# Groups of eight heads in a ring of three 8 MiB slots: fewer, longer loads for a decode attention block that streams its cache

## The chip, the cores and the metric

One core of one Trainium2 chip. The metric is device time in microseconds (us), the median of several executions; lower is better.

## The reference, cut to what matters

Eight requests, one new token each. An attention block over a cache (32 heads, 4096 positions, 128 values per head) and an MLP (576 to 4608 to 576) run on the same input and are mixed by a gate.

```python
q = (x @ wq)                      # (8, 1, 576) @ (576, 4096), 32 heads of 128
scores = einsum("bhqd,bhkd->bhqk", q, k_cache) * 128 ** -0.5
p = softmax(scores)
a = einsum("bhqk,bhkd->bhqd", p, v_cache).reshape(8, 1, 4096) @ wo
b = gelu(layernorm(x) @ w1 + b1) @ w2 + b2
out = g * a + (1 - g) * b         # g = sigmoid(sum(x * gate_w))
```

K and V are 268 MB each, in bf16, and every byte is used once. The weights are another 20 MB.

Of the kernel before, what the change touches and what calls it, by code (L numbers as in the profile page):

```python
# [21 lines left out]
HB = 4  # L22
NHG = H // HB
NG = NHG * B
NTT = SK // 32
# [4 lines left out]
TQ = 4  # L30
QN = D // 4
QP = 96 + B
NTQ = NTT // TQ
# [51 lines left out]
def bass_gated_mix__mha_block_cached__mixer_channel_mlp__decode_kernel(  # L85
# [32 lines left out]
    KB = [sb(f"KB{i}", [128, NTT, DH], BF16) for i in range(2)]  # L118
    VB = [sb(f"VB{i}", [128, NTT, DH], BF16) for i in range(2)]
    RB = sb("RB", [128, 9 * F // 2], BF16)  # L120
    wq_sb = view(RB, 0, [128, 4, SK])
    wq_t = view(RB, 4 * SK, [128, SK // 2])
    w1_sb = view(RB, 0, [128, 4, F])
    w1_t = view(RB, 4 * F, [128, F // 2])
    w2_sb = view(RB, 0, [128, NJ, D])
    wo_sb = view(RB, 0, [128, H, D])
    p1 = sb("p1", [128, 2, CT, DH], BF16)

    pos = [0]

    def early(shape):
        n = int(np.prod(shape[1:]))
        ap = view(p1, pos[0], shape)
        pos[0] += n
        assert pos[0] <= 2 * CT * DH
        return ap

    x_sb = early([B, D])
    gw8 = early([B, D])
    y_sb = early([B, D])  # L140
    junk = early([B, D])
    xz = early([B, 2, 64, 2])
    yz = early([B, 2, 64, 2])
    xT_sb = early([128, NKF + 2, B])
    yT_sb = sb("yT_sb", [128, NKF + 2, B], BF16)
    b1_sb = sb("b1_sb", [128, NJ], BF16)
    b2_4 = sb("b2_4", [128, QN], BF16)
    hT_sb = sb("hT_sb", [128, NJ, B], BF16)
    up = sb("up", [128, 2, NJ * B], F32)
    Q4 = sb("Q4", [128, NHG * DH], BF16)  # L150
    Sel = sb("Sel", [128, B, 128], BF16)
    q_bc = sb("q_bc", [128, 2, DH], BF16)
    OT_sb = sb("OT_sb", [128, H, B], BF16)
    bmg_sb = view(up, 0, [128, QN])
# [3 lines left out]
    ones = sb("ones", [128, 128], F32)  # L158
    sel16 = sb("sel16", [128, TQ, HB], F32)
# [5 lines left out]
    mD = sb("mD", [128, 2, 32], F32)  # L165
    gm = sb("gm", [128, 1], F32)
    P = sb("P", [128, 2, NTT, HB], BF16)
    rs = sb("rs", [128, 2, HB], F32)
    O_sb = sb("O_sb", [128, TQ, DH], F32)
    rz = sb("rz", [128, HB], F32)  # L170
# [7 lines left out]
    up_ps = bank[6]  # L178
    y_ps = bank[7]
    YT_COL = 64  # L180

    sK = [nc.alloc_semaphore(f"sK{i}") for i in range(2)]
    sV = [nc.alloc_semaphore(f"sV{i}") for i in range(2)]
    nK, nV = [0, 0], [0, 0]
# [8 lines left out]
    def bcast(t):  # L193
        return bass.AP(tensor=t.tensor, offset=t.offset, ap=[[0, B], [1, D]])

    c_b2 = op("gpsimd", lambda e: e.memset(b2_4[:], 0.0))
    c_g4 = op("gpsimd", lambda e: e.memset(g4[:], 0.0))
    ld_x = load("sync", x_sb, x_flat, "ld_x")
    ld_gw = load("scalar", gw8, bcast(gate_w), "ld_gw")
    ld_b2 = [load("scalar", b2_4[32 * i:32 * i + B, :],  # L200
                  bass.AP(tensor=B_b2.tensor, offset=B_b2.offset + i * QN, ap=[[0, B], [1, QN]]), f"ld_b2{i}", [c_b2])
             for i in range(4)]
    ld_b1 = load("scalar", b1_sb[:, :], B_b1.rearrange("(p j) -> p j", j=NJ), "ld_b1")
    def halves(w):
# [3 lines left out]
    ld_wq = [load("sync", wq_sb, A_wq[0:512, :].rearrange("(kt p) n -> p kt n", p=128), "ld_wqa"),  # L208
             load("sync", wq_t, halves(A_wq), "ld_wqb")]


    def kv_src(cache, g):
        hg, b = divmod(g, B)
        return cache[b, hg * HB:(hg + 1) * HB].rearrange("h (p t) d -> (h p) t d", p=32)

    k_done, v_done = {}, {}
    k_land, v_land = {}, {}

    def load_k(g):
        s = g % 2  # L220
        nK[s] += 1
        src = kv_src(A_k_cache, g)
        k_land[g] = op("sync", lambda e: e.dma_start(KB[s][:, :, :], src), [k_done.get(g - 2)], dma=(sK[s], 16 * nK[s]))  # L223

    def load_v(g):
        s = g % 2
        nV[s] += 1
        src = kv_src(A_v_cache, g)
        t = op("sync", lambda e: e.dma_start(VB[s][:, :, :], src), [v_done.get(g - 2)], dma=(sV[s], 16 * nV[s]))  # L229
        v_land[g] = [(t, 0, NTT)]  # L230

    V_LAST = (32, 32, 16, 16, 16, 8, 8)

    def load_v_pieces(g):
        s = g % 2
        src = kv_src(A_v_cache, g)
        v_land[g] = []
        t0 = 0
        for n, nt in enumerate(V_LAST):
            dst, part = VB[s][:, t0:t0 + nt, :], src[:, t0:t0 + nt, :]  # L240
            t = load("sync", dst, part, f"sVl{n}", [v_done.get(g - 2)])
            v_land[g].append((t, t0, t0 + nt))
            t0 += nt
        assert t0 == NTT

    load_k(0)
    load_v(0)
    load_k(1)


    def memset(engine, ap, value):
# [7 lines left out]
    c_ones = memset("gpsimd", ones[:], 1.0)  # L259
    c_mA = memset("gpsimd", mA[:], 0.0)  # L260
    c_P = memset("gpsimd", P[:], 0.0)
    c_ps = [memset("vector", bank[i][:, :], 0.0) for i in range(4)]
    c_yps = memset("vector", y_ps[:, :], 0.0)
    c_sel16 = op("vector", lambda e: e.tensor_reduce(
        out=sel16[:].rearrange("p t h -> p (t h)"),
# [3 lines left out]
        out=Sel[:].rearrange("p b (h r) -> p b h r", h=HB),  # L269
        in_=bass.AP(tensor=ident, offset=0, ap=[[pstride(ident), 128], [1, B], [32, HB], [0, 32]])), [c_id])  # L270
# [24 lines left out]
    def transposed(src, srcz, col, waits):  # L295
        last = None
        for kt in range(NKF + 2):
            o = up_ps[:, col + kt * B:col + (kt + 1) * B]
            i = src[:, kt * 128:(kt + 1) * 128] if kt < NKF else srcz[:, kt - NKF, :, :].rearrange("b r s -> b (r s)")
            last = op("tensor", lambda e, o=o, i=i: e.matmul(o, lhsT=i, rhs=ident[0:B, 0:B], start=True, stop=True),  # L300
                      waits if kt == 0 else ())
        return last

    def untransposed(dst, col, waits):
        return op("vector", lambda e: e.tensor_copy(
            out=dst.rearrange("p k b -> p (k b)"), in_=up_ps[:, col:col + (NKF + 2) * B]), waits)

    v_xz = spread(xz, x_sb, [ld_x])
    p_xT = transposed(x_sb, xz, 0, [ld_x, c_id, v_xz])
# [11 lines left out]
    v_yT = untransposed(yT_sb[:, :, :], YT_COL, [p_yT])  # L321
# [3 lines left out]
    for half in range(2):  # L325
        for h in range(HB):
            for kt in range(NKT):
                o = tr_ps[half][32 * h:32 * h + B, :]
                at = (kt * SK + half * (SK // 2) if kt < NKF else NKF * SK) + h * DH
                r = bass.AP(tensor=RB, offset=at, ap=[[pstride(RB), 128], [HB * DH, 4], [1, DH]])  # L330
# [6 lines left out]

    ld_w1 = [load("sync", w1_sb, B_w1[0:512, :].rearrange("(kt p) f -> p kt f", p=128), "ld_w1a", [p_Q]),
             load("sync", w1_t, halves(B_w1), "ld_w1b")]


    a_qb, v_mult, v_red, p_sum, v_nm, a_exp, p_pv, a_ev, p_oz, v_norm, v_rs, p_z, v_rz = ({} for _ in range(13))

    def q_of(g):
        hg, b = divmod(g, B)
        t = op("tensor", lambda e: e.matmul(qb_ps[:, 0:DH], lhsT=Sel[:, b, :], rhs=Q4[:, hg * DH:(hg + 1) * DH],  # L346
                                            start=True, stop=True), [a_Q[hg // 4], c_Sel, a_qb.get(g - 1)])
        a_qb[g] = op("scalar", lambda e: e.activation(out=q_bc[:, g % 2, :], in_=qb_ps[:, 0:DH], func=ACT.Copy),  # L348
                     [t, v_mult.get((g - 2, NCK - 1))])

    def mult(g, c):
        s, par = g % 2, c % 2
        qb = bass.AP(tensor=q_bc, offset=q_bc[:, s, :].offset, ap=[[pstride(q_bc), 128], [0, CT], [1, DH]])
        v_mult[g, c] = op("vector", lambda e: e.tensor_tensor(  # L354
            out=p1[:, par, :, :], in0=KB[s][:, c * CT:(c + 1) * CT, :], in1=qb, op=ALU.mult),
            [k_land[g], a_qb[g], p_sum.get((g, c - 2) if c >= 2 else (g - 1, c + NCK - 2))]
            + ([v_yT, p_yT, p_Q] if g == 0 and c < 2 else []))
        if c == NCK - 1:
            k_done[g] = v_mult[g, c]
        for n in range(NCH):  # L360
            r = bass.AP(tensor=p1, offset=p1[:, par, 0, n * CH:n * CH + 1].offset,
                        ap=[[pstride(p1), 128], [DH, CT], [1, CH]])
            w = [v_mult[g, c], v_red.get((g, c - 2) if c >= 2 else (g - 1, c + NCK - 2)), *a_Q] if n == 0 else ()
# [21 lines left out]
    def softmax(g):  # L385
# [4 lines left out]
        t = op("vector", lambda e: e.tensor_reduce(out=gm[:, :], in_=mB[:, :], axis=AX.X, op=ALU.max), [t])  # L390
        gmb = bass.AP(tensor=gm, offset=0, ap=[[pstride(gm), 128], [0, 32]])
        t = op("vector", lambda e: e.tensor_scalar(out=mC[:, :], in0=gmb, scalar1=-1.0, scalar2=None, op0=ALU.mult), [t])
        v_nm[g] = op("vector", lambda e: e.transpose(mD[:, s, :], mC[:, :]), [t, a_exp.get(g - 2)])  # L393
        for h in range(HB):
            q = slice(32 * h, 32 * h + 32)
            a_exp[g] = op("scalar", lambda e, h=h, q=q: e.activation(  # L396
# [118 lines left out]
    def norm_turned(g):  # L515
# [3 lines left out]
            [p_oz[g], v_rz[g]])  # L519


    UP0, UPN = 3, 12
    DN0, DNN = 19, 6
    AP0 = 28
    q_of(0)
# [107 lines left out]
```

## The kernel before: the parts that the change touches

A group is one request and four heads: 4 MiB of K and 4 MiB of V, in which each of the 128 partitions holds one contiguous row of 32 KiB (128 positions of one head). K and V have two buffers each, and the weights pass one after the other through a fifth buffer.

```python
HB = 4                                   # heads of a group
KB = [sb(f"KB{i}", [128, NTT, DH], BF16) for i in range(2)]
VB = [sb(f"VB{i}", [128, NTT, DH], BF16) for i in range(2)]
RB = sb("RB", [128, 9 * F // 2], BF16)   # wq, then w1, w2, wo
p1 = sb("p1", [128, 2, CT, DH], BF16)    # products of K and q, two chunks
def load_k(g):                           # waits until the products of group g-2 are done
    ...
    op("sync", lambda e: e.dma_start(KB[s][:, :, :], src), [k_done.get(g - 2)], ...)
V_LAST = (32, 32, 16, 16, 16, 8, 8)      # the last V comes in seven pieces
```

Scores are made in chunks of 32 positions per partition: VectorE multiplies the chunk by the query into `p1`, TensorE adds up 8 slices of 16 values with an identity matrix, and VectorE reduces the remaining 16. Softmax, the value product on TensorE, and the normalisation follow, spread over the next groups' chunks by `between`.

```python
def mult(g, c):
    v_mult[g, c] = op("vector", ... tensor_tensor(out=p1[:, par, :, :], in0=KB[s][...], in1=qb, op=ALU.mult) ...)
    for n in range(NCH):                 # 8 matmuls of 512 columns
        ... matmul(tr_ps[par][:, :], lhsT=ident[:, :], rhs=r, ...)
def between(c, g=g):
    if c == 1 and g >= 1:
        rowsum(g - 1)                    # VectorE: sums of the exponentials
        ...
```

## Time and profile before

| | before |
|---|---|
| time, median of the 3 runs made first | 1310.3 us |
| span of the profile | 1308.8 us |
| bytes read | 557 MB, 426 GB/s over the span |
| busy: TensorE / VectorE / ScalarE | 64% / 66% / 16% |

These are lines of the page of the kernel before: the DMA rows of the 40 equal slices of the span (busy share in tenths, then GB/s), and the first lines of its chain of waits.

```profile
DMA  9999999999999999999999999999999999999997
GB/s 398 422 431 432 431 432 431 432 431 430 434 424 432 430 431 429 428 418 432 429 431 429 431 431 431 431 432 430 432 430 431 431 431 429 432 431 432 429 420 311
...
DMA 69%; DVE 20%; PE 10%; SPq 0%; issue 0%; ACT 0%
```

The loads bound the kernel. The DMA engines are busy in nearly every slice, at a rate that hardly moves. Compute engines have a third of their time to spare, so work taken from them is worth nothing by itself. What can be won is in the rate of the stream, its gaps, its start and its end.

This is the view by windows for the kernel before: each row is a stretch in us, then its length, then busy time and instruction counts of PE, PEld, DVE, ACT and POOL, then the granted clock (the share of TensorE's full clock that it was given), the DMA share and GB/s. The view counts a packet wholly in the stretch in which it starts, so a share can come out a little wrong, and even above 1.

```profile
core 0: us, PE busy (x) PEld busy (x) DVE busy (x) ACT busy (x) POOL busy (x), PEclk, DMA share, GB/s
1284.00:1286.00 2.00, 2.00 (x8) 0.68 (x7) 1.38 (x3) 0.00 (x0) 0.00 (x0) 0.62 0.99 426
1286.00:1288.00 2.00, 2.00 (x16) 0.77 (x18) 2.00 (x2) 0.00 (x0) 0.00 (x0) 1.00 0.84 360
1288.00:1290.00 2.00, 2.00 (x31) 0.81 (x24) 2.00 (x3) 0.47 (x1) 0.00 (x0) 1.00 0.53 221
1290.00:1292.00 2.00, 1.61 (x9) 0.57 (x7) 2.00 (x2) 0.13 (x1) 0.00 (x0) 1.00 0.79 291
1292.00:1294.00 2.00, 2.00 (x14) 1.27 (x12) 0.61 (x2) 0.00 (x0) 0.00 (x0) 1.00 0.92 373
```

The DMA share falls to 0.53. The prediction below comes to this dip.

### The profile page before, as it was taken

How to read it: one execution, taken by the hardware profiler on the slowest of the kernel's cores; microseconds unless marked ns; L12 is line 12 of the kernel's file. 1: busy time of each engine (PE TensorE's matmuls, PEld its weight loads, DVE VectorE, ACT ScalarE, POOL GpSimd, SP SyncE). 2: the span in 40 equal slices, each digit the busy share in tenths (PEclk: the TensorE clock that was granted, in tenths of full speed). 3: DMA queues.
4: the chain of work that ended last, by engine and by line, in shares of the span. 5: the costliest groups of instructions: out<-in, count | busy, mean ns of one | idle time of the engine just before them, and what ended most of it. 6: DMA issues, size and time to landing. Idle time of an engine off the chain costs nothing.

```text
span 1308.8 us, 12641 instructions
## 1 busy us (share of the span) xinstructions
PE 843.5 (64%) x5428; PEld 384.4 (29%) x5428; DVE 869.7 (66%) x1061; ACT 204.1 (16%) x393; POOL 2.5 (0%) x13
## 2 busy tenths in 40 slices
PE   3567766766746666646766766765766665766766
PEld 1223433433312233212322222322322222322323
DVE  4576676676747667646766766766776666776675
ACT  1201111111210110101011111011111111111111
POOL 0000000000000000000000000000000000000000
PEclk8878888878868888768878878878878878878878
DMA  9999999999999999999999999999999999999997
GB/s 398 422 431 432 431 432 431 432 431 430 434 424 432 430 431 429 428 418 432 429 431 429 431 431 431 431 432 430 432 430 431 431 431 429 432 431 432 429 420 311
DMA packets 25255, 557.77 MB, mean 426 GB/s; under 512 B 2528, under 2 KB 6640, under 8 KB 7536
## 3 DMA queue, kind: packets, MB, share of 16 engines
q1 hardware_dynamic: 24944, 556.95, 99.4%
q8 instruction: 42, 0.69, 0.2%
q14 instruction: 13, 0.11, 0.0%
q10 hardware_dynamic: 256, 0.03, 0.0%
HBM read 556.96 MB, written 0.01 MB: 426 GB/s over the span
## 4 chain that ended last, share of the span: by engine, by line
DMA 69%; DVE 20%; PE 10%; SPq 0%; issue 0%; ACT 0%
DMA KB<-in_A_k_cache_dram 68%; DVE p L354 16%; PE psb L364 10%; DVE s_sb L369 3%; DMA VB<-in_A_v_cache_dram 1%; SPq L187 0%; PE psb L414 0%; ACT L467 0%; SPq L229 0%; DVE mA L387 0%; SPq L223 0%; PE psb L477 0%; DVE mB L389 0%; ACT O_sb L427 0%; DVE gm L390 0%
## 5 line engine op out<-in xcount | busy, mean ns | idle before, releaser
L364 PE MATMUL psb<-p,ident 128*128 128x512 bf16 x2048 | 610.9, 459 | 412.2 <-DVE p L354 411.8
L354 DVE TENSOR_TENSOR p<-KB,q_bc 128x4096 bf16<-128x4096 bf16 x256 | 579.6, 2285 | 278.0 <-DMA KB<-in_A_k_cache_dram 278.0
L364 PEld LDWEIGHTS psb<-p,ident 128*128 128x128 bf16 x2048 | 218.1, 114 | 744.5 <-DVE p L354 445.2
L369 DVE TENSOR_REDUCE s_sb<-psb 128x32 f32<-128x512 f32 x256 | 176.1, 688 | 129.9 <-PE psb L364 129.6
L427 ACT ACTIVATE O_sb<-psb 128x512 f32<-128x512 f32 x63 | 37.6, 597 | 1032.2 <-PE psb L414 1032.2
L396 ACT ACTIVATE P<-s_sb,mD 32x128 bf16<-32x128 f32 x256 | 147.0, 574 | 12.9 <-DVE mD L393 9.0
L414 PE MATMUL psb<-VB,P 128*16 128x512 bf16 x2016 | 119.9, 379 | 0.3 <-DMA VB<-in_A_v_cache_dram 0.3
L432 PE MATMUL psb<-sel,O_sb 128*128 128x4 f32 x504 | 66.9, 256 | 32.9 <-ACT O_sb L427 32.9
L432 PEld LDWEIGHTS psb<-sel,O_sb 128*128 128x128 f32 x504 | 61.6, 192 | 41.3 <-ACT O_sb L427 41.2
L414 PEld LDWEIGHTS psb<-VB,P 128*16 128x16 bf16 x2016 | 44.7, 89 | 70.4 <-issue 26.3
L402 DVE TENSOR_REDUCE rs<-P 128x4 f32<-128x512 bf16 x64 | 43.5, 680 | 2.1 <-ACT P L396 2.1
L421 PEld LDWEIGHTS psb<-rs,ones 128*128 128x128 f32 x128 | 24.4, 192 | 9.3 <-issue 0.4
L348 ACT ACTIVATE q_bc<-psb 128x128 bf16<-128x128 f32 x64 | 17.4, 272 | 32.7 <-PE psb L346 32.7
L452 PEld LDWEIGHTS psb<-yT_sb,RB 128*128 128x128 bf16 (+1 forms) x216 | 19.4, 165 | 3.4
L452 PE MATMUL psb<-yT_sb,RB 128*128 128x8 bf16 (+1 forms) x216 | 19.8, 227 | 0.0
L387 DVE TENSOR_REDUCE mA<-s_sb 128x1 f32<-128x128 f32 x64 | 18.3, 286 | 2.2
L421 PE MATMUL psb<-rs,ones 128*128 128x4 f32 x128 | 18.4, 214 | 0.0
L389 DVE STREAM_TRANSPOSE mB<-mA 128x32 f32<-128x32 f32 x64 | 13.6, 213 | 2.2
L393 DVE STREAM_TRANSPOSE mD<-mC 128x32 f32<-128x32 f32 x64 | 13.6, 212 | 2.2
L346 PE MATMUL psb<-Q,Sel 128*128 128x128 bf16 x64 | 14.7, 229 | 0.0
L346 PEld LDWEIGHTS psb<-Q,Sel 128*128 128x128 bf16 x64 | 6.1, 96 | 27.0 <-issue 26.8
L390 DVE TENSOR_REDUCE gm<-mB 128x1 f32<-128x32 f32 x64 | 11.9, 186 | 2.2
(63 smaller groups left out, 84.7 us busy)
## 6 DMA issues: line engine op xcount, KB each, us to landing
KB<-in_A_k_cache_dram SPq DMA_DIRECT2D x64, 4096.0 KB, 27.2
VB<-in_A_v_cache_dram SPq DMA_DIRECT2D x63, 4096.0 KB, 33.1
RB<-in_B_w_dram SPq DMA_DIRECT2D x1, 5184.0 KB, 44.3
RB<-in_B_w_dram SPq DMA_DIRECT2D x1, 4608.0 KB, 36.6
RB<-in_A_wo_dram SPq DMA_DIRECT2D x1, 4608.0 KB, 44.7
RB<-in_A_wq_dram SPq DMA_DIRECT2D x1, 4096.0 KB, 12.8
VB<-in_A_v_cache_dram SPq DMA_DIRECT2D x2, 1024.0 KB, 8.7
VB<-in_A_v_cache_dram SPq DMA_DIRECT2D x3, 512.0 KB, 11.2
```

The source lines that it names most:

```text
L346: t = op("tensor", lambda e: e.matmul(qb_ps[:, 0:DH], lhsT=Sel[:, b, :], rhs=Q4[:, hg * DH:(hg + 1) * DH], start=True, stop=True), [a_Q[hg ...
L354: v_mult[g, c] = op("vector", lambda e: e.tensor_tensor(out=p1[:, par, :, :], in0=KB[s][:, c * CT:(c + 1) * CT, :], in1=qb, op=ALU.mult), ...
L364: p_sum[g, c] = op("tensor", lambda e, r=r, n=n: e.matmul(tr_ps[par][:, :], lhsT=ident[:, :], rhs=r, start=(n == 0), stop=(n == NCH - 1)), w)
L369: v_red[g, c] = op("vector", lambda e: e.tensor_reduce(out=s_sb[:, s, c * CT:(c + 1) * CT], in_=tr_ps[par][:, :].rearrange("p (t c) -> p t ...
L387: t = op("vector", lambda e: e.tensor_reduce(out=mA[:, 0:1], in_=s_sb[:, s, :], axis=AX.X, op=ALU.max), [v_red[g, NCK - 1], c_mA])
L396: a_exp[g] = op("scalar", lambda e, h=h, q=q: e.activation(out=P[q, s, :, h], in_=s_sb[q, s, :], func=ACT.Exp, bias=mD[q, s, 0:1], scale=1.0),
L402: v_rs[g] = op("vector", lambda e: e.tensor_reduce(out=rs[:, s, :], in_=P[:, s, :, :].rearrange("p t h -> p h t"), axis=AX.X, op=ALU.add), ...
L414: p_pv[g] = op("tensor", lambda e, o=o, tq=tq: e.matmul(o, lhsT=P[:, s, tq * TQ:(tq + 1) * TQ, :].rearrange("p t h -> p (t h)"), rhs=VB[s] ...
L421: p_z[g] = op("tensor", lambda e: e.matmul(oz_ps[:, HB:2 * HB], lhsT=ones[:, :], rhs=rs[:, g % 2, :], start=True, stop=True), [v_rs[g], v_ ...
L427: a_ev[g] = op("scalar", lambda e: e.activation(out=O_sb[:].rearrange("p t d -> p (t d)"), in_=o_ps[s][:, :], func=ACT.Copy), [p_pv[g], p_ ...
L432: p_oz[g] = op("tensor", lambda e, tt=tt: e.matmul(oz_ps[:, 0:HB], lhsT=O_sb[:, tt, :], rhs=sel16[:, tt, :], start=(tt == 0), stop=(tt == ...
L452: st["p_up"] = op("tensor", lambda e, w=w, o=o, kt=kt: e.matmul(o, lhsT=w, rhs=yT_sb[:, kt, :], start=(kt == 0), stop=(kt >= NKF)), [*ld_w ...
```

## The change

Intent: a group takes eight heads, so that a row is 64 KiB and a load 8 MiB, half as many and twice as long. To have room for that, K, V and all weights share one ring of three 8 MiB slots, and the product of K and the query is written over K in place. The MLP is done first, while the first K and V stream in. wo is loaded last. The diff, cut to its core:

```diff
-HB = 4
+HB = 8
-    KB = [sb(f"KB{i}", [128, NTT, DH], BF16) for i in range(2)]
-    VB = [sb(f"VB{i}", [128, NTT, DH], BF16) for i in range(2)]
-    RB = sb("RB", [128, 9 * F // 2], BF16)
-    p1 = sb("p1", [128, 2, CT, DH], BF16)
+    SL = sb("SL", [128, 3 * SLOT], BF16)
+    slot = [view(SL, i * SLOT, [128, NTT, DH]) for i in range(3)]
...
+    def load_kv(kind, g):
+        n = n_load[0]
+        s = n % 3
+        ...
+        land[kind, g] = op("sync", lambda e: e.dma_start(slot[s][:, :, :], src), free[n - 3], dma=(sS[s], 16 * nS[s]))
...
-        v_mult[g, c] = op("vector", ... tensor_tensor(out=p1[:, par, :, :], in0=KB[s][...], in1=qb, op=ALU.mult),
+        v_mult[g, c] = op("vector", ... tensor_tensor(out=part, in0=part, in1=qb, op=ALU.mult),
...
         def between(c, g=g):
-            if c == 1 and g >= 1:
+            if g >= 1 and c == 1:
                 rowsum(g - 1)
...
         scores(g, between)
+        free[n_of["k", g]] = [p_sum[g, NCK - 1]]
+        if g < NG - 1:
+            next_load()
+        else:
+            load_wo(free[n_of["k", g]])
+        if g >= 1:
+            pv(g - 1)
+            free[n_of["v", g - 1]] = [p_pv[g - 1]]
+            next_load()
         softmax(g)
+        if g >= 1:
+            evict(g - 1)
```

The loads come in the order K0, K1, V0, K2, V1, K3, V2 and so on. Load n waits for the slot of load n-3. The probabilities `P` have one buffer instead of two, so the exponentials of a group wait for the value product of the group before.

## The prediction

> **What bounds the kernel now.** The loads. The page's slice rows show the DMA engines 90% or more busy in 39 of 40 slices, at 430 to 432 GB/s in most; PE is busy 64%, DVE 66%. The DMA view gives 557 MB in a span of 1308.8 us. In the trace's packet records a 32 KiB packet takes 1.216 us on one of 16 engines (431 GB/s in all), back to back from about 3.4 to 1304.5 us. The Trainium skill, "DMA: Bandwidth & Descriptors", section "Where 436 GB/s comes from", states a ceiling of 435; this trace agrees. So streaming has under 1% left, and compute saved is off the path: DVE waits 278 us for K loads (waits view).
>
> Not at full rate: 3 us before the first packets; 4096 wo packets of 1152 B (13.1 us per engine instead of about 11); near the end two 2 us stretches at 74% and 57%, where the last V's pieces wait for an earlier product (1.5 us lost), then small V packets; 4.3 us from the last packet to the end.
>
> **What the change does.** Same bytes.
> - 64 KiB rows: from packets of 32768 B (1.216 us) and 41472 B (1.538 us) I estimate 2.428 us for 65536 B, against 2.432 for two of 32 KiB: 2 us saved.
> - wo in rows of 4608 B: 1.5 to 2 us saved. wq, w1 in long rows: under 1 us.
> - Last V whole, no dip: 1.5 to 2 us saved; wo (about 11.5 us) streams last and hides the last product with V.
> - Longer tail: after the last wo bytes come gather, normalise, transpose and 32 output matmuls; I estimate 5.7 us instead of 4.3.
> - Per group of eight heads: 8 chunks of 2.28 (product) + 0.69 (reduce) plus about 4: 28 us DVE per two loads (38.9 us). The exponentials took 0.57 us for 128 columns; at 256 I estimate 1 us, 8 us per group on ACT: it fits.
> - Ring of three: a K slot must be free within two loads of landing. Scores take about 27 us, slack 11, so the queue should never run dry.
> - MLP first: w1 lands about 27 us, up about 6, gelu 4, 144 small transposes 8, down 4 to 10: done near 55 us; its slot is wanted about 78, and K of group 0 lands about 59. No bubble; least slack about 4 us, for the second K's slot, about 115 us.
>
> **Sum.** Start 3 us, packets about 1292, tail about 5.7: span about 1301, time (1.5 above the span, as before) about 1303 us, 0.6% faster.
>
> Predicted 1303 us, 8 in 10 between 1298 and 1309. Faster by over 2%: 0.02. Within 2%: 0.93. Slower by over 2%: 0.05.
>
> **What would show it.** K and V packets of 65536 B at 2.42 to 2.44 us; slices at 430 to 433 GB/s with no dip at wo or near the end; wo packets of 4608 B; a chain of waits that ends in wo; DVE waiting for K about 10 us per group; MLP done before 60 us.
>
> **What would make it wrong.** (1) 64 KiB rows put the engines' streams 512 KiB apart instead of 256; the same page ("Latency and other measured facts") reports much slower copies at some power-of-two row pitches. No trace here shows it; if it strikes, packets exceed 2.5 us and the time rises several per cent. (2) Slots freed late: three buffers only, and in-place products hold K until the last PE sum; each 1 us missed per group costs 32 us. (3) The MLP ends after 78 us. (4) The tail chain runs over 8 us.

## The result, and the profile after

| | before | after |
|---|---|---|
| time, median (lowest to highest) | 1310.5 us (1310.3 to 1310.7, 4 runs) | 1307.5 us (1307.0 to 1307.7, 4 runs) |
| span of the profile | 1308.8 us | 1305.3 us |
| first byte of the large loads to the last | 1.7 to 1304.3 us | 1.8 to 1300.8 us |
| last byte to the end | 4.6 us | 4.5 us |
| typical K/V packet | 32 KiB, 1.216 us | 64 KiB, 2.421 us |
| mean granted TensorE clock | 0.82 | 0.85 |

The ratio is 0.9977 with a 95% interval of 0.9963 to 0.9991. The change is 3.0 us faster where 7 were predicted. The measured time lies in the predicted range, but only because the range was wide: less than half of the forecast gain came.

These lines of the page after answer to those of before: the DMA rows of the slices, and the head of the chain of waits.

```profile
DMA  9998999999999999999999999999999999999997
GB/s 392 437 440 376 436 432 433 433 432 434 428 440 426 437 432 432 436 426 441 422 443 424 441 424 437 430 438 426 440 424 441 424 440 427 438 431 432 432 436 299
...
DMA 53%; DVE 30%; PE 13%; ACT 4%; issue 0%; SPq 0%; ACTq 0%
```

There is a dip that was not there before: 376 GB/s in the fourth slice, 98 to 131 us. In the view by windows no packet starts in it from 116 to 120 us (same columns as above):

```profile
112.00:114.00 2.00, 1.62 (x9) 0.59 (x7) 2.00 (x2) 0.28 (x1) 0.00 (x0) 1.00 0.68 295
114.00:116.00 2.00, 1.66 (x8) 0.70 (x8) 2.00 (x3) 0.00 (x0) 0.00 (x0) 1.00 1.14 492
116.00:118.00 2.00, 1.10 (x6) 0.41 (x5) 1.69 (x2) 0.00 (x0) 0.00 (x0) 1.00 0.00 0
118.00:120.00 2.00, 2.00 (x25) 0.85 (x27) 0.89 (x2) 0.00 (x0) 0.00 (x0) 1.00 0.00 0
```

The trace also has every DMA packet. By these records the engines ran dry one after the other, from 116.2 to 118.2 us, and began again from 120.0 to 120.9 us; all 16 stood still together for 1.9 us. A load ends with 16 small packets, one for each engine, so their times tell when each engine was done with it. For the loads around the dip:

```
load   first engine done   last engine done   since the load before
K0          58.2                60.1               19.7
K1          77.5                79.5               19.3
V0          96.9                98.8               19.4
K2         116.2               118.2               19.4
V1         139.9               141.4               23.3
K3         159.2               160.8               19.4
```

An 8 MiB load takes 19.35 us when the stream is full. V1 is 3.9 us late, and nothing later makes up for it. V1 needs the slot of K1. This is the timeline of the kernel after for the scores of group 1 on VectorE and ScalarE (start, duration, engine, line, operation; in brackets the idle time before it and what ended it):

```profile
87.45 4.48 DVE L437 TENSOR_TENSOR SL<-SL,q_bc 128x4096 bf16<-128x4096 bf16 x2
87.58 9.42 ACT L477 ACTIVATE P<-s_sb,hb 128x256 bf16<-128x256 f32 x8 [6.21 <-DVE hb L474]
97.03 2.29 DVE L482 TENSOR_REDUCE rr<-P 128x1 f32<-128x2048 bf16 x1 [5.09 <-ACT P L477]
99.23 0.68 DVE L447 TENSOR_REDUCE s_sb<-psb 128x32 f32<-128x512 f32 x1
```

VectorE makes two products of group 1 and then stands idle for 5.1 us. Its next instruction is the row sum of group 0 (L482), which needs all eight exponentials of group 0 (L477), and these take 9.4 us. K1 has been there since 79.5 us. The engine that frees the slot is blocked by an instruction that has nothing to do with the slot. The waits view of the kernel after shows that this happens only four times (total us, times, longest). By the timeline these are groups 1 to 4, with 5.1, 6.4, 3.0 and 1.5 us, and only the first of them made a load late:

```profile
DVE SL L437 <- DMA SL<-in_A_k_cache_dram: 255.3, 29, 10.9
...
DVE rr L482 <- ACT P L477: 15.9, 4, 6.4
```

The same packet records show a second thing. The spread between the first and the last of the 16 engines at the end of a load grows through the run: 1.5 us at V1, 3.5 us near 550 us, 7.7 us at 1270 us. At the end, with the last of wo, seven engines were done by 1293.1 to 1295.1 us and nine only by 1299.1 to 1300.7 us. The average engine finished at 1297.1 us, 3.7 us before the last.

### The profile page after: what moved, and what is told of

Same layout as the page of the kernel before. It is cut to its first block, busy times and chain, and to the rows that moved or that the text cites. A ratio compares the mean times of both kernels' runs of the same rounds, so it can differ in the third digit from the quotient of the medians. Undisturbed runs are those within 1.5% of the kernel's fastest.

```text
span 1305.3 us, 11677 instructions
## 1 busy us (share of the span) xinstructions
PE 739.7 (57%) x5136; PEld 302.2 (23%) x5136; DVE 880.3 (67%) x860; ACT 329.6 (25%) x330; POOL 3.8 (0%) x19
## 4 chain that ended last, share of the span: by engine, by line
DMA 53%; DVE 30%; PE 13%; ACT 4%; issue 0%; SPq 0%; ACTq 0%
DMA SL<-in_A_k_cache_dram 51%; DVE SL L437 21%; PE psb L442 6%; PE psb L492 5%; DVE s_sb L447 5%; ACT P L477 4%; DVE rr L482 3%; DMA SL<-in_A_wo_dram 2%; PE psb L510 1%; DMA SL<-in_A_wq_dram 1%; DVE Orow L517 0%; PE psb L355 0%; DVE rz L516 0%; PE psb L506 0%; PE psb L406 0%
## 5 line engine op out<-in xcount | busy, mean ns | idle before, releaser
L442 PE MATMUL psb<-SL,ident 128*128 128x512 bf16 x2048 | 559.8, 426 | 521.4 <-DVE SL L437 521.4
L437 DVE TENSOR_TENSOR SL<-SL,q_bc 128x4096 bf16<-128x4096 bf16 x256 | 581.5, 2282 | 267.1 <-DMA SL<-in_A_k_cache_dram 255.3
L442 PEld LDWEIGHTS psb<-SL,ident 128*128 128x128 bf16 x2048 | 200.9, 107 | 855.2 <-DVE SL L437 608.2
L477 ACT ACTIVATE P<-s_sb,hb 128x256 bf16<-128x256 f32 x256 | 299.9, 1602 | 296.1 <-PE psb L492 289.9
L492 PE MATMUL psb<-SL,P 128*32 128x512 bf16 x2048 | 118.2, 383 | 0.0
L482 DVE TENSOR_REDUCE rr<-P 128x1 f32<-128x2048 bf16 x32 | 73.0, 2280 | 16.0 <-ACT P L477 15.9
L492 PEld LDWEIGHTS psb<-SL,P 128*32 128x32 bf16 x2048 | 54.2, 97 | 60.9 <-issue 13.1
L510 PE MATMUL psb<-O_sb,sel 128*8 128x128 f32 x256 | 34.4, 279 | 9.9 <-ACT O_sb L498 9.9
L510 PEld LDWEIGHTS psb<-O_sb,sel 128*8 128x8 f32 x256 | 21.2, 91 | 14.5 <-ACT O_sb L498 10.0
L465 DVE TENSOR_REDUCE mA<-s_sb 128x1 f32<-128x256 f32 x32 | 13.4, 420 | 1.1
```

Source lines behind the costliest of these rows:

```text
L437: v_mult[g, c] = op("vector", lambda e: e.tensor_tensor(out=part, in0=part, in1=qb, op=ALU.mult), [land["k", g], a_qb[g]])
L442: p_sum[g, c] = op("tensor", lambda e, r=r, n=n: e.matmul(tr_ps[par][:, :], lhsT=ident[:, :], rhs=r, start=(n == 0), stop=(n == NCH - 1)), w)
L465: t = op("vector", lambda e: e.tensor_reduce(out=mA[:, 0:1], in_=s_sb[:, s, :], axis=AX.X, op=ALU.max), [v_red[g, NCK - 1], c_mA])
L477: a_exp[g] = op("scalar", lambda e, h=h: e.activation(out=P[:, :, h], in_=s_sb[:, s, :], func=ACT.Exp, bias=hb8[:, h:h + 1], scale=1.0), [ ...
L482: v_rs[g] = op("vector", lambda e: e.tensor_reduce(out=rr[:, g % 2:g % 2 + 1], in_=P[:, :, :].rearrange("p t h -> p (t h)"), axis=AX.X, op ...
L492: p_pv[g] = op("tensor", lambda e, o=o, tq=tq: e.matmul(o, lhsT=P[:, tq * TQ:(tq + 1) * TQ, :].rearrange("p t h -> p (t h)"), rhs=vb[:, tq ...
```

## The experiments

Two things had to be explained: the 3.9 us gap, and the slow drift of the engines. The first theory is the blocked row sum; its rivals are that three slots are too few in any case, or that the MLP delays the first scores. For the drift, one suspect is the instruction fetches: the records of the DMA engines also hold packets of the kind "instruction", 40 of 16 KiB in TensorE's queue in the kernel after and some of 8 KiB in another. The other suspect is engines or memory places that differ in speed. A third question is what the 64 KiB rows are worth alone. Each experiment was timed against the kernel before in the same rounds; that one's median was between 1310.5 and 1310.6 us in every set, so medians of different sets can be compared to about 0.2 us. The three sets (e1 to e4, e5 to e7, e8 to e10) ran on three chips.

### e1: the row sum later

```diff
-            if g >= 1 and c == 1:
+            if g >= 1 and c == 5:
                 rowsum(g - 1)
```

> Only the row sum moves, from the second to the sixth chunk of the next group's scores. Theory (in the first groups, where K has already landed, VectorE stands idle in the row sum until the eight exponentials of the group before are done, so the second K's slot is freed late and the queue runs dry for 3.9 us): the gap in the load completions between the fifth and the sixth K/V load shrinks from 23.3 to 19.4 us, and the time falls by 3 to 4 us against the changed kernel, to about 1303.8 us. Rival (three slots are too few whatever VectorE does, or the MLP holds up the first scores): the gap stays, and the time stays within 1 us of 1307.5.

Measured: 1305.06 us (1304.6 to 1306.2, 5 runs), 2.5 us faster than the change. V1 came 19.8 us after K2 instead of 23.3. So the gap was made by the blocked row sum and not by the three slots or the MLP. The time gained less than the gap, and the runs scattered over 1.6 us: something else now had a part in the end. In the profile, the end came 5.8 us after the last byte instead of 4.5.

### e2: more instructions on TensorE

e1 with each value product cut in two of 256 columns.

```diff
-            p_pv[g] = op(... o, lhsT=P[...], rhs=vb[:, tq * TQ:(tq + 1) * TQ, :] ...)
+            for u in range(2):
+                p_pv[g] = op(... o[:, 256 * u:256 * u + 256], lhsT=P[...], rhs=vb[:, tq * TQ + 2 * u:tq * TQ + 2 * u + 2, :] ...)
```

> e1 with each of the 2048 value products on TensorE cut into two of 256 columns: same arithmetic and same K and V bytes, 4096 more TensorE instructions. Theory (the instruction fetches take about 1 us each on the same nine or ten of the 16 DMA engines, so these fall behind the other six, and the end is set by the slowest): about 16 more fetch packets of 16 KiB, the spread of the 16 engines at the last K/V load grows from about 7.6 to 9.5 to 11 us, and the time is 1.5 to 3 us above e1. Rival (the spread comes from engines that differ in speed or from where the rows lie in memory): spread within 0.7 us of that of e1, time within 0.5 us of e1 unless the first groups stall again.

Measured: 1309.22 us, 4.2 us slower than e1, with 16 more fetch packets of 16 KiB. The direction is the theory's and the size is above it. The spread did not grow as expected: it was 5.9 us at the last K/V load and 4.8 at the one before, because the engines that were ahead ran out of freed slots (the first engine's completions came up to 2.4 us late in five loads). As the end also came 6.3 us after the last byte, e2 does not separate the fetches from the extra work on TensorE. It was repeated as e9 on a cleaner base.

### e3: half rows

e1 with every K/V load issued as two loads of half the positions.

```diff
+        for u in range(2):
+            nS[s] += 1
+            ts = slice(u * NTT // 2, (u + 1) * NTT // 2)
+            ... e.dma_start(slot[s][:, ts, :], src[:, ts, :]) ...
```

> e1 with each K/V load issued as two of 4 MiB, so the packets are 32 KiB again and everything else is as in e1. If longer packets are worth what the two traces say (2 x 1.216 against 2.421 us a packet, 512 packets an engine): 4 to 6 us slower than e1. By the estimate in the prediction (2.432 against 2.428): 2 us slower. If the length of a packet does nothing: 0.

Measured: 1310.35 us, 5.3 us slower than e1, as the packets' durations say and more than the prediction's 2 us. But its end came 6.8 us after the last byte, so part of that may be the end. It was repeated as e10.

### e4: which engines are late

e1 with a tiny load of 2 to 14 rows behind each K/V load. The Trainium skill, "DMA: Bandwidth & Descriptors", section "Why a DMA increments its semaphore by 16 and not by 1", says that a load over fewer rows runs on the lowest-numbered engines. The trace has one packet for each row of these loads, as that asks, but no record shows an engine's number.

```diff
+        mark_at[i] = op("sync", lambda e: e.dma_start(mark[0:kk, i, 0:w], A_wq[0:kk, 0:w]), ...)
```

> e1 with a tiny load of 2 to 14 rows behind each K/V load, which by the page on DMA uses only the lowest-numbered engines; the moment of its packets tells which engines are the late ones. Theory: the same six engines are ahead in all loads. If the low-numbered ones are ahead, the marks of 2 to 6 rows come with the first completions of their load; if they are behind, 6 us after the first. Time within 1 us of e1.

Measured: 1307.12 us in the one execution, 2 us above e1, so the expected 1 us was missed. The markers worked: each came within 0.03 us of a completion of its load. At the last marked loads, the 2-row marker sat 0.5 and 2.1 us behind the first engine, the 4-row marker added one engine near the first and one 4.8 us behind, and the 6-row marker again one of each. So both readings fail: if the page is right about the numbers, the low-numbered engines are neither the early nor the late ones, but mixed. Bytes can then not be shifted to the early ones by the number of rows alone.

### e5: the last value products earlier

e1 with the value product of the last group but one, and its eviction, ahead of the last chunk of scores.

```diff
+            if c == 6 and g == NG - 1:
+                pv(g - 1)
+                evict(g - 1)
```

> e1 with, in the last group only, the value product of the group before and its eviction moved ahead of the last chunk of scores, so that the last exponentials (9.4 us) start about 1.7 us earlier and the last value product no longer waits behind a gather that waits for the eviction. Theory (in e1 the last value product starts at 1289.8 us although its data landed about 1285.7, and the output products end about 2 us after the last wo piece): the last value product starts about 2.5 us earlier, the time falls by 1.5 to 2 us against e1, and then the wo loads end the kernel. Rival (the wo loads already end it): within 0.5 us of e1.

Measured: 1306.84 us, with runs from 1303.8 to 1307.9. A miss: not faster than e1. The profiled run (the slowest, 1307.9) shows why. The product did not wait for V, which had landed at 1268.7 us; it ran from 1276.0 to 1279.6 us. But TensorE works in order, and now the sums of the last chunk come behind the product, from 1279.6 us, and VectorE's maximum behind them. In e1 the maximum was made while the product ran. So the last exponentials started at 1283.9 us instead of 1279.2. Part of that is chance in this run: K31 landed 1.8 us later, and the sums before the product took 3.4 us instead of 1.9, at a granted clock of 0.50. Work moved forward in an in-order queue delays what it passes by its own length.

### e6: the row sum last

e1 with the row sum behind the last product, so that it delays neither the slot nor anything that the slot waits for.

```diff
-            if g >= 1 and c == 5:
+            if g >= 1 and c == 7:
                 rowsum(g - 1)
```

> e1 with the row sum behind the last product instead of the sixth, so that each K slot comes free about 2.3 us earlier. In e1 the engines that run ahead were short of work three times (0.5 to 1.8 us) because no slot was free for them. If the slowest engines set the end: the engines ahead get further ahead (spread at the last K/V load 7 to 9 us instead of 5.5), and the time stays within 0.7 us of e1. If the ring's slack sets it: faster by 1.5 us or more.

Measured: 1303.19 us (1303.17 to 1303.36, 5 runs), 1.9 us faster than e1, 4.3 us faster than the change, and 0.9944 of the kernel before (0.9930 to 0.9957). It is the fastest version that computes the reference. The expectation does not decide it: by its time the rival won (faster by over 1.5 us), by its spread the theory (7.9 us at the last K/V load, and the first engine no longer late there). Both left out the end of the kernel, and the profiles of e1 and e6 show it. The last K/V byte came at 1285.7 us in e1 and 1285.6 in e6, the last byte of all at 1297.1 and 1296.9, so the stream was no faster. But from the last byte to the end it took 5.8 us in e1 and 4.5 in e6. This is e1, then e6, with the row sum of the last group but one, its value product, the start of the last group's exponentials (eight in all, but the views end at 1281 us), and the last line of the chain of waits:

```profile
1265.64 2.28 DVE L482 TENSOR_REDUCE rr<-P 128x1 f32<-128x2048 bf16 x1
...
1275.40 3.64 PE L492 MATMUL psb<-SL,P 128*32 128x512 bf16 x64
...
1279.15 2.56 ACT L477 ACTIVATE P<-s_sb,hb 128x256 bf16<-128x256 f32 x2 [28.67 <-PE psb L492]
...
1290.43 4.71 PE psb L492 x54
```

```profile
1270.98 2.28 DVE L482 TENSOR_REDUCE rr<-P 128x1 f32<-128x2048 bf16 x1
1272.95 3.64 PE L492 MATMUL psb<-SL,P 128*32 128x512 bf16 x64
...
1276.70 4.83 ACT L477 ACTIVATE P<-s_sb,hb 128x256 bf16<-128x256 f32 x4 [29.18 <-PE psb L492]
...
1273.48 21.11 DMA SL<-in_A_wo_dram
```

In e1 the row sum sits ahead of the last two products, so the last exponentials start 2.5 us later, and the chain from the last K to the output ends after the wo loads: it closes with the last value product. In e6 it ends with the loads. A group of eight heads has twice the latency of a group of four, and at the end of the kernel that latency is no longer hidden unless it fits under V30, V31 and wo.

The dip is gone too. These windows of e6 answer to those of the kernel after:

```profile
114.00:116.00 2.00, 2.00 (x44) 0.93 (x36) 1.60 (x7) 0.00 (x0) 0.00 (x0) 1.00 1.14 492
116.00:118.00 2.00, 0.29 (x8) 0.00 (x0) 0.00 (x0) 1.60 (x2) 0.00 (x0) 1.00 0.99 426
118.00:120.00 2.00, 0.00 (x0) 0.00 (x0) 1.33 (x1) 2.00 (x3) 0.00 (x0) 0.97 1.01 434
```

### e7: fewer instructions

e5 with half of the value products left out in all but the last two groups. The result is wrong on purpose; the check of results let e7 and e8 pass all the same, so it does not show that a version computes the reference.

```diff
-        for tq in range(NTQ):
+        for tq in range(NTQ) if g >= NG - 2 else [t for t in range(NTQ) if t % 8 < 4]:
```

> e5 with half of the value products left out in all but the last two groups (a wrong result on purpose): about 1900 TensorE instructions fewer, 7 or 8 fetch packets of 16 KiB fewer, same bytes of K, V and weights. Theory (each fetch holds one of nine or ten DMA engines for about 1 us and the slowest sets the end): 0.8 to 2 us faster than e5. Rival (fetches do not matter; e2 was slower because of the extra work on TensorE): within 0.4 us of e5.

Measured: 1305.69 us, 1.2 us faster than e5, with 8 fetch packets of 16 KiB fewer. That is what was expected, but both kernels scatter over 3 to 4 us, so it is inconclusive. It was repeated as e8.

### e8 and e9: fewer and more fetches on a clean base

e6 ends with its loads and repeats within 0.2 us. e8 is e6 with the edit of e7 (wrong), and e9 is e6 with the edit of e2 in all but the last two groups.

> e6, whose end is set by the wo loads and whose runs agree within 0.2 us, with half of the value products left out in all but the last two groups (a wrong result on purpose): 8 fetch packets of 16 KiB fewer, the same loads. Theory (a fetch holds one DMA engine for about 1 us, the nine or ten late engines share them, the latest sets the end): 0.7 to 1.6 us faster than e6, and the lag of the last engine behind the first at the last K/V load 0.8 to 1.6 us smaller. Rival (fetches cost nothing; e2 was slow by its work on TensorE): within 0.3 us of e6.

> e6 with the value products of all but the last two groups cut into two of 256 columns: 15 fetch packets of 16 KiB more, the same loads, the last two groups unchanged. Theory: 1.3 to 3 us slower than e6, most of it in the lag of the last engine behind the first, as long as the first does not wait for slots. Rival: within 0.3 us of e6.

Measured: e8 1302.39 us (1302.3 to 1302.6), 0.8 us faster than e6. e9 1306.19 us (1306.1 to 1306.6), 3.0 us slower. Both lie at the edge of what was expected, the one at its small end, the other at its large end. The page's line for the queue that brings TensorE's instructions (packets, MB, share of the 16 engines) is, for e8, e6 and e9 in turn:

```profile
q8 instruction: 32, 0.52, 0.2%
```

```profile
q8 instruction: 40, 0.66, 0.2%
```

```profile
q8 instruction: 55, 0.90, 0.3%
```

In the packet records, the first engine was done with the last K/V load at 1277.7 us in e8 and in e6, and the last engine at 1284.8 us in e8, 1285.6 in e6 and 1289.0 in e9. The lag of the last behind the first was 7.1, 7.9 and 8.5 us. The end followed the last byte by 4.5 us in all three. So the fetches cost time although their share of all engines is 0.2%, and the latest engine carries it: 0.1 us for each fetch from 32 to 40, 0.2 us for each from 40 to 55. e8 has less work on TensorE too, but no part of it was in the way in e6. In e9 the lag grew by 0.6 us only, and not by most of the 3.0 us, as was expected: the first engine waited up to 1.3 us for slots in three late loads and came 2.8 us later than in e6. The last engine had no such wait; in those loads it came 19.35 to 19.39 us after the load before.

The records also show what one fetch costs. In e6, from V1 to the last K/V load but one, 41 K/V packets took more than 0.1 us over the typical 2.42 us, and each of the 41 starts where an instruction packet ends (32 of 16 KiB, 9 of 8 KiB). The instruction packet of 16 KiB takes 1.07 us there and the K/V packet behind it about 0.5 us more than others, so by these records a fetch of 16 KiB costs its engine about 1.5 us. All 41 together come to 58 us, while the 16 engines' lags behind the first grew by 50 us in sum. No other packet was long, so the fetches are enough to make the drift. Fifteen fetches more, shared by nine engines, would be 2.5 us an engine by this estimate, near the 3.0 us of e9.

### e10: half rows on a clean base

e6 with the edit of e3.

> e6 with each K/V load issued as two of 4 MiB (32 KiB packets). e3 gave 5.3 us over e1, but both had ends that the last group's work had a part in. If the packets' own durations are the reason (1.216 against half of 2.421, 1024 packets of 32 KiB an engine): 5 to 6.5 us slower than e6, and the extra time is spread evenly over the whole run. If part of e3's loss came from the end: 2 to 4 us.

Measured: 1307.93 us (1307.85 to 1307.96, 5 runs), 4.7 us slower than e6, just below the expected 5 to 6.5. The last byte came 5.0 us later than in e6 and the end 4.1 us after it, so this time nothing but the stream was longer. The loss is spread evenly: 2.6 us at 685 us, 4.9 at 1267 us. The 64 KiB rows are worth 4.7 us here, more than twice the prediction's 2.

## Why the prediction was right or wrong

The kernels line up as a chain. Before: 1310.5. The whole change with 32 KiB packets and the row sum out of the way (e10): 1307.9. With 64 KiB packets (e6): 1303.2. With the row sum where the change has it: 1307.5. The change wins about 7.3 us and gives 4.3 of it back in a wait. What the first 2.6 us come from (the longer packets of the weights, the order of the loads, the last V in one piece, the end) was not separated.

**The step that failed: "Ring of three: ... Scores take about 27 us, slack 11, so the queue should never run dry", and with it "No bubble; least slack about 4 us, for the second K's slot".** The prediction named the right slot, the second K's, and the right moment, but its time for the scores was a sum of VectorE's busy times (8 x 2.97 us and about 4). It left out that VectorE waits inside the scores. The row sum at the second chunk waits for eight exponentials, 9.4 us, and in the first groups, where K has landed before the scores begin, nothing hides that. The slot came free about 8 us later than worked out (near 119 us where it was wanted by 115), and the next load was 3.9 us late. These lines are the issue of that load, V1, in the kernel after and in e6:

```profile
119.07 0.33 SPq L259 DMA_DIRECT2D SL<-in_A_v_cache_dram  x1
```

```profile
112.75 0.33 SPq L259 DMA_DIRECT2D SL<-in_A_v_cache_dram  x1
```

So 6.3 of the 8 us are the row sum, its wait and its own 2.3 us. Moving one line gives 4.3 us back (after against e6), and the measured e6, 1303.2 us, is what the prediction said for the change.

**That agreement is partly luck.** The sum of the prediction was start 3, packets 1292, tail 5.7. The kernel after measured 1.8, 1298.9 and 4.5.
- *Packets about 1292.* The average engine was done 1295.3 us after the first byte. Without the gap of 3.9 us that is 1291.4, as predicted, though the longer rows saved more than predicted (next point), so another term of the sum was too small by about as much; which one is open. And the kernel waits for the last engine, 3.7 us behind the average. The prediction averaged over 16 engines that do not finish together. e8 and e9 show that fetches make that lag longer, and the records of e6 that they are enough to account for it.
- *64 KiB rows: 2 us saved.* They saved 4.7 (e10 against e6). The estimate went through two packet sizes below 64 KiB and gave 2.428 us; the packets took 2.421 us. The difference of 7 ns is small, but each engine takes 512 of them: 3.6 us.
- *Start 3 and tail 5.7.* Both were 1.2 us too long.

**What the prediction read wrongly in the profile before.** "Two 2 us stretches at 74% and 57%, where the last V's pieces wait for an earlier product (1.5 us lost)". The wait was there: the seven pieces were issued at 1289.5 us, when the value product before them was done.

```profile
1287.58 1.90 PE L414 MATMUL psb<-VB,P 128*16 128x512 bf16 x32
...
1289.53 3.77 SPq L187 DMA_DIRECT2D VB<-in_A_v_cache_dram  x7
```

But by the packet records it cost only seven of the 16 engines anything: they were done by 1287.2 to 1287.9 us and got the first pieces at 1290.6 us. The other nine worked on the load before until 1292.2 to 1294.2 us and went on to the pieces without a pause. Only the slowest engine's loss counts, so by this reading taking the dip away could win nothing; no run tested it on the kernel before. It was there to be seen: the share does not go to 0, as it does in the gap of the kernel after.

**What was right.** The loads bound both kernels; compute moved off the path; the MLP caused no delay, as V0 came 19.4 us after K1; wo came in packets of 4608 B (2304 B in its last two pieces); the end is a chain that closes with wo. The danger of slow power-of-two row pitches did not come true with rows of 64 KiB: 2.421 us a packet, faster than two of before. The exponentials were estimated at 8 us a group on ScalarE and took 9.4, which "fits" as busy time; it was their latency that counted.

**What stays open.** Why the fetches come on nine or ten engines and leave six alone is not known (in e6 the first six engines were within 0.4 us of one another at the last K/V load but one, so none of them can have had a fetch more than the others); e4 shows only that early and late engines are mixed among the low numbers, if the page on their order is right. The lag that would be left without fetches was not measured.

## What to carry to other kernels

When a ring of slots feeds a stream, work out when a slot comes free from the order of the instructions on the engine that frees it, with each one's wait, and do it for the first rounds too, where the data is there early and hides nothing. In this kernel an instruction that waits for another engine was worth moving behind the last one that frees a slot (4.3 us). When transfers are the bound, as here, the last of the DMA engines sets the end, so look at the spread of their completions and not only at the mean rate; and a few nanoseconds a packet are microseconds at the end of a stream.

## What the Trainium skill lacked or had wrong

- "Runtime: NRT & Kernel Launch", section "Instruction fetch mechanics", says that crossing a 16 KiB boundary costs one DMA tail-bump, mostly hidden. In a kernel bound by loads it was not hidden: the record of a fetch packet of 16 KiB lasted 1.05 us on one DMA engine (mean of 40 in the kernel after), the K/V packet behind it about 0.5 us longer than others, 15 packets more went with 3.0 us more (e9), 8 fewer with 0.8 us less (e8).
- No page says which DMA engines bring instructions, or that they fall behind the others: here the 16 engines drifted from 1.5 to 7.7 us apart over 1130 us.
- "DMA: Bandwidth & Descriptors", section "Measured", whose loads are issued from GpSimd, stops at 425 GB/s for 16 MB and does not say what longer rows bring. Here 32 KiB packets ran at 431 GB/s and 64 KiB packets at 433 GB/s (65536 B in 2.421 us on each of 16 engines), which is nearer to the 435 that its section "Where 436 GB/s comes from" gives as the ceiling of the ports of the on-chip memory. The same section says that for loads from HBM a limit of about 358 binds; with one core at work, these loads ran above it. The step was worth 4.7 us of 1308.
- The same page, section "Latency and other measured facts", warns of row pitches at large powers of two, measured on copies between memory tensors with rows of 16 KiB. Here loads of 64 KiB rows that lie one behind the other were not slower: 2.421 us a packet. The pitches that the page lists were not tried, so it stays untested.
